# Block 0 of a retention layer prepared by pairs of heads, block 1's scores moved into the first product, and block 3's queries scaled on another engine

## The chip, the cores and the metric

The kernel runs on one core of one Trainium2 chip. The metric is the device time of one execution in microseconds (us). A core has a matrix engine (TensorE, PE in the profile; its weight loads are PEld), a vector engine (VectorE, DVE), a scalar engine (ScalarE, ACT), a general engine (GpSimd, POOL) and SyncE (SP), which here only issues DMAs. Each engine runs its instructions in the order in which they were written; between engines, semaphores make an instruction wait for its inputs.

## What is computed

A retention layer (attention without softmax, with a decay by distance) over 8 batches, 8 heads, 576 tokens and head size 64, and behind it a two-layer perceptron with `h * cos(h)` between its layers:

```python
scores = scale * np.matmul(q, k.transpose(0, 1, 3, 2))
gamma = 1.0 - 2.0 ** (-5.0 - np.arange(H, dtype=np.float32))
Dmat = np.where(rel >= 0, gamma[:, None, None] ** rel[None, :, :], 0.0)
attn = np.matmul(scores * Dmat[None], v)          # rel = query position - key position
x = attn.transpose(0, 2, 1, 3).reshape(B * S, H * D)   # 4608 x 512
h = x @ w_in                                      # 512 x 2048
out = (h * np.cos(h)) @ w_out                     # 2048 x 512
```

## The kernel before

The 4608 tokens are cut into 18 **blocks** of 256 (`BK`), numbered j. A **tile** n of the perceptron has 512 tokens, so blocks 2n and 2n+1. The decay is split into a factor for the query and one for the key (`gq`, `gkp`, `gkc`), so that a block needs a causal mask only, plus a running state `s_all` that carries key-times-value sums from earlier tokens. For one block the steps are:

- `load` (L132): q, k and v come as three float32 tiles `fq`, `fk`, `fv` by DMAs on SP's queue. The pool has three buffers of each.
- `scaled` (L163): one tensor-times-tensor per half y of the block multiplies q or k by its factors and rounds to bf16 (`qks`); `prep` (L188) does all four on POOL. `round_v` (L181) rounds v (`vb`).
- `turned` (L196) or, for blocks 0 and 1, `transpose_pe` (L218): PE turns `qks` into a PSUM bank, and ACT or DVE copies it out ("evacuates" it) to `qkT`.
- `scores` (L249): 32 small matmuls give query-key products in PSUM; two `masked` steps on DVE multiply them by the mask into `ret`.
- `sums_of` (L321): PE forms the key-value sums; the function that it returns adds them to the running state on DVE (`s_all`, L380 and L384), and the function which that one returns rounds the state on ACT (`sb`, L394).
- `out_own` (L404) and `out_carried` (L441): PE adds the block's own part (from `ret` and `vb`) and the carried part (from `sb`); ACT rounds the result to `xT`, the input of the perceptron.

The perceptron's first layer is `mm1` (L479): groups of PE matmuls h, a cosine on ACT (`cosh`, L503) and a multiplication on DVE (`gT`, L506). The dictionary `inside` (L924) names work that is put on PE's queue between such groups. For tile 0 the second layer is the loop at L988; for tiles 1 to 8 it is `mm2_seven` (L628), which saves one of eight quarter products by sums and differences of operands; `w_sums` (L518, `ws`) forms the differences of `w_out` on DVE, each 128x1024 in bf16, during tile 0's second layer.

The weights come by DMAs that POOL issues and that round float32 to bf16 on the way: `load_w_in` four times (512 columns each, L741), `load_w_out` four times (L747). `w_dma` numbers them 0 to 7, and `after` makes one DMA wait until another has landed.

**The order of the work is written by hand.** Three places matter here:

- The start, L760 to L870: loads of blocks 0 and 1 (v of block 1 waits until k of block 1 has landed, L763), tables and masks, block 0 up to `xT`, then block 1's transposes and its scores, and then the first product. `warm(n, tag)` (L232) puts n matmuls on zeros onto PE's queue to keep it busy. Block 2's loads wait for `w_dma[3]` (L846), and block 3's for `w_dma[6]` (L869).
- Tile 0's first layer, L891 to L937: eight groups of 16 matmuls. The second needs the second load of `w_in`, the third the third.
- Tile 0's second layer, L964 to L1002: `todo` lists work with the number of the matmul ahead of which it is queued, and is sorted by it. Number 28 is `turned(2)`, 34 to 36 are `ws` 6, 4 and 7 (first halves), 40 block 2's scores and masks, 41 its state, 42 `prep(3)`, 51 to 53 the second halves of the three `ws`, 54 `outputs(2)`, 55 the rounding of block 3's v on ACT, 60 `turned(3)`. Block 3's scores then stand inside tile 1's first product (L926).

Of the kernel before, what the change touches and what calls it, by code (L numbers as in the profile page):

```python
# [8 lines left out]
F32 = mybir.dt.float32  # L9
BF16 = mybir.dt.bfloat16  # L10
# [7 lines left out]
def kernel(  # L18
# [143 lines left out]

    def scaled(eng, j, name, y):  # L163
        f = tiles["f" + name, j]
        if ("qks", j) not in tiles:
            tiles["qks", j] = nat.tile([P, 2, 2, HG, 2, D], BF16, tag="qks", name="qks")
        dst = tiles["qks", j][:, "qk".index(name), y]
        if name == "q" or j < NP_B:
            src = f[:, :, y, :]
            by = (gq if name == "q" else gkp)[:, j % PERQ, y, :]  # L170
        else:
            src = f[:, y]
            by = gkc[:, (2 * j + y) % PERK, :]
        return eng.tensor_tensor(  # L174
            out=dst.rearrange("p b a d -> p a b d"),
            in0=src.rearrange("p (a b) d -> p a b d", a=2),
            in1=by.rearrange("p (a b) -> p a b", a=2).unsqueeze(3).to_broadcast([P, 2, HG, D]),
            op=ALU.mult,
        )
# [69 lines left out]
    def scores(j, banks):  # L249
        cs = chunks[j]  # L250
        kT = tiles["qkT", j]
        ret = retp.tile([P, 2, HG, 2, P], BF16, tag="ret", name="ret")
        if cs[0].pair:
            pss = [
                psum.tile([P, HG, 2, P], F32, tag=t, name="sc")
                if isinstance(t, str)
                else [psum.tile([P, HG, P], F32, tag=u, name="sc") for u in t]
                for t in banks
            ]
            order = [(c, y, he, hg) for hg in range(HG) for y in range(2) for he in range(2) for c in cs]  # L260
            mask = mask_p
            for c, y, he, hg in order:
                ps = pss[he]
                nc.tensor.matmul(
                    ps[y][c.rows, hg, :] if isinstance(ps, list) else ps[c.rows, hg, y, :],
                    lhsT=kT[he * D : he * D + D, 1, y, hg, c.rows],
                    rhs=q_cols(c, he, hg, c.n),
                    start=True,
                    stop=True,
                )  # L270

            def masked(he):
                if isinstance(pss[he], list):
                    for y in range(2):
                        nc.vector.tensor_tensor(
                            out=ret[:, he, :, y, :],
                            in0=pss[he][y],
                            in1=mask[:, y].unsqueeze(1).to_broadcast([P, HG, P]),
                            op=ALU.mult,
                        )  # L280
                    return
                nc.vector.tensor_tensor(  # L282
                    out=ret[:, he].rearrange("p b r i -> p b (r i)"),
                    in0=pss[he].rearrange("p b r i -> p b (r i)"),
                    in1=mask.rearrange("p r i -> p (r i)").unsqueeze(1).to_broadcast(
                        [P, HG, 2 * P]
                    ),
                    op=ALU.mult,
                )
# [28 lines left out]
        tiles["ret", j] = ret  # L318
# [442 lines left out]
    k1 = load(1, "k")  # L761
    load(1, "q")
    load(1, "v", gate=k1)  # L763
# [22 lines left out]
    warm(11, "n")  # L786
# [115 lines left out]

    def block1_sums():
        sums_of(1, "st")()()
# [16 lines left out]
    for n in range(NT):  # L921
        blocks = blocks_of.get(n) or [(e + k * E2, 0, W) for e in range(0, E2, 2) for k in range(2)]
        for i, (et, c0, cw) in enumerate(blocks):
            inside = {  # L924
                (0, 1): {2: block1_carried},
# [33 lines left out]
        if n == 0:  # L959
# [10 lines left out]
                (42, lambda: prep(3)),  # L970
# [17 lines left out]
            for done, (t, e) in enumerate(order):  # L988
# [9 lines left out]
                for u in range(2 * (t == 1) if t < 2 else 1) if e == ET - 1 else ():  # L998
# [3 lines left out]
                    stores.append((u * P, ot))  # L1002
            continue
# [115 lines left out]
```

## Time and profile before

| | |
|---|---|
| median of three runs | 296.96 us (296.85 to 297.02) |
| the profiled execution: its time, and its span in the profile | 296.85 us, 295.1 us |
| busy: PE, PEld, DVE, ACT, POOL | 284.5, 196.3, 215.2, 170.5, 143.4 us |
| chain of work that ended last, by engine | PE 83%, DVE 5%, ACT 3%, DMA 3%, POOL 2% |
| DMA, 10 to 30 us from the span's start | busy share 1.2 of 16 engines, about 205 to 255 GB/s |
| granted TensorE clock | 1.00 in every stretch |

The span is the stretch that the profile covers; about 1.75 us of the execution lie outside it. Times in the views below are counted from the span's start. A row of the timeline has the start, the length, the engine, the line, the operation, output and inputs, the number of instructions that it merges, and in brackets the idle time before it with what ended it. A row of DMA issues ends with the size and the time from issue to landing.

### The profile page before, as it was taken

To read this page: it belongs to the slowest core of one execution; us is meant where nothing else is said; L and a number is where in the kernel's file an instruction comes from. 1 tells how busy PE (TensorE), PEld (TensorE's weight loads), DVE (VectorE), ACT (ScalarE), POOL (GpSimd) and SP (SyncE) were. 2 spreads that over 40 slices of the span, in tenths; PEclk is the share of its full clock that TensorE was granted. 3 is DMA by queue.
4 is the path that set the end of the run, shared out by engine and by line. 5 is a ranking of instruction groups with operands and counts; after the bars stand their busy time and mean duration, and the time that the engine had idled before them with its cause. 6 is when DMAs were issued, how large, how long until landed. Compare 5 with 4: busy or idle time off the path is not lost.

```text
span 295.1 us, 10506 instructions
## 1 busy us (share of the span) xinstructions
PE 284.5 (96%) x4367; PEld 196.3 (67%) x4388; DVE 215.2 (73%) x300; ACT 170.5 (58%) x200; POOL 143.4 (49%) x163
## 2 busy tenths in 40 slices
PE   7899999999999999999999999999999999999994
PEld 2578545878864687468745884588458845884584
DVE  5756767758857887698769866986698669745943
ACT  3676317476558844767476737674768466535620
POOL 8621439970585995349434942495249014102400
PEclk9999999999999999999999999999999999999999
DMA  7999999999989857833873396429201130112013
GB/s 222 289 206 224 227 251 233 260 231 221 227 189 232 218 134 173 201 71 98 213 189 77 78 225 176 100 52 257 58 0 40 38 73 0 40 47 62 2 36 107
DMA packets 103981, 42.62 MB, mean 144 GB/s; under 512 B 68480, under 2 KB 103424, under 8 KB 103936
## 3 DMA queue, kind: packets, MB, share of 16 engines
q1 hardware_dynamic: 99184, 37.37, 51.8%
q0 software_dynamic: 4224, 4.19, 8.7%
q8 instruction: 36, 0.59, 0.9%
q10 hardware_dynamic: 528, 0.39, 0.4%
q14 instruction: 9, 0.07, 0.1%
HBM read 36.70 MB, written 9.44 MB: 156 GB/s over the span
## 4 chain that ended last, share of the span: by engine, by line
PE 83%; DVE 5%; ACT 3%; DMA 3%; POOL 2%; SPq 1%; issue 1%; ACTq 0%; DVEq 0%
PE h L490 41%; PE o L610 32%; PE ov L420 3%; PE tr L210 2%; POOL qks L174 2%; DMA fq<-in_q_dram 2%; PE ov L447 1%; PE sc L302 1%; DMA fk<-in_k_dram 1%; DVE gT L506 1%; PE st L335 1%; ACT cosh L503 1%; SPq L153 1%; DVE qks L174 1%; DVE ret L282 1%
## 5 line engine op out<-in xcount | busy, mean ns | idle before, releaser
L490 PE MATMUL h<-xT,w_in_sb 128*128 128x512 bf16 (+1 forms) x689 | 126.8, 340 | 1.3 <-DVE qkT L216 0.4
L506 DVE TENSOR_TENSOR gT<-h,cosh 128x1024 bf16<-128x1024 f32 x72 | 87.7, 1222 | 33.5 <-ACT cosh L503 33.1
L490 PEld LDWEIGHTS <-w_in_sb 128*128 128x128 bf16 x704 | 68.1, 98 | 55.2 <-issue 1.1
L503 ACT ACTIVATE cosh<-h,half_pi 128x1024 f32<-128x1024 f32 x72 | 79.9, 1115 | 40.5 <-PE h L490 40.5
L549 POOL TENSOR_TENSOR gs<-gT 128x512 bf16<-128x512 bf16 x28 | 35.8, 1277 | 100.4 <-DVE gT L506 100.4
L610 PEld LDWEIGHTS <-gs 128*128 128x128 bf16 x528 | 49.7, 98 | 5.9
L610 PEld LDWEIGHTS <-gT 128*128 128x128 bf16 x384 | 36.6, 98 | 6.1
L636 DVE TENSOR_TENSOR ot<-ot,o 128x512 f32<-128x512 f32 x35 | 23.2, 683 | 22.4 <-ACT ot L640 14.2
L174 POOL TENSOR_TENSOR qks<-fk,gkc 128x512 bf16<-128x512 f32 x32 | 37.1, 1178 | 2.8 <-DMA fk<-in_k_dram 2.8
L174 POOL TENSOR_TENSOR qks<-fq,gq 128x512 bf16<-128x512 f32 x31 | 34.7, 1137 | 7.5 <-DMA fq<-in_q_dram 7.5
L216 ACT COPY qkT<-tr 128x1024 bf16<-128x1024 bf16 x29 | 27.7, 1022 | 6.4 <-PE tr L210 6.4
L394 ACT CAST sb<-s_all 128x768 bf16<-128x768 f32 (+2 forms) x18 | 16.3, 904 | 25.6 <-DVE s_all L384 21.6
L610 PE MATMUL o<-w_out_sb,gs 128*128 128x256 bf16 (+1 forms) x264 | 30.6, 269 | 0.1
L610 PE MATMUL o<-w_out_sb,gT 128*128 128x256 bf16 x256 | 30.6, 273 | 0.0
L610 PE MATMUL o<-ws,gs 128*128 128x256 bf16 (+1 forms) x264 | 30.5, 269 | 0.0
L640 ACT COPY ot<-o 128x512 f32<-128x512 f32 x33 | 19.3, 584 | 16.0 <-PE o L610 16.0
L311 DVE TENSOR_TENSOR ret<-sc,mask_c 128x512 bf16<-128x512 f32 x32 | 20.7, 685 | 7.3 <-PE sc L302 7.3
L185 POOL CAST vb<-fv 128x512 bf16<-128x512 f32 x31 | 19.3, 646 | 4.8 <-DMA fv<-in_v_dram 4.8
L466 ACT CAST xT<-ov 128x1024 bf16<-128x1024 f32 x16 | 16.2, 1012 | 9.4 <-PE ov L447 9.2
L384 DVE TENSOR_TENSOR s_all<-st,s_all 128x256 f32<-128x256 f32 x49 | 20.7, 422 | 1.2
L549 DVE TENSOR_TENSOR gs<-gT 128x512 bf16<-128x512 bf16 (+1 forms) x25 | 16.7, 668 | 0.5
L610 PE MATMUL o<-ws,gT 128*128 128x256 bf16 x128 | 15.3, 273 | 0.0
(73 smaller groups left out, 207.0 us busy)
## 6 DMA issues: line engine op xcount, KB each, us to landing
out_dram<-ot SPq DMA_DIRECT2D x68, 128.0 KB, 2.6
fk<-in_k_dram SPq DMA_DIRECT2D x28, 256.0 KB, 4.9
fv<-in_v_dram SPq DMA_DIRECT2D x28, 256.0 KB, 4.8
fq<-in_q_dram SPq DMA_DIRECT2D x12, 512.0 KB, 5.1
w_in_sb<-in_moe_w_in_dram POOLq DMA_DIRECT2D x4, 512.0 KB, 8.0
w_out_sb<-in_moe_w_out_dram POOLq DMA_DIRECT2D x4, 512.0 KB, 8.3
fq<-in_q_dram SPq DMA_DIRECT2D x4, 384.0 KB, 5.1
fk<-in_k_dram SPq DMA_DIRECT2D x2, 512.0 KB, 4.9
```

What stands on the lines that cost most here:

```text
L174: return eng.tensor_tensor(out=dst.rearrange("p b a d -> p a b d"), in0=src.rearrange("p (a b) d -> p a b d", a=2), in1=by.rearrange("p (a ...
L185: runs[y](vb[:, y], f[:, :, y, :] if j < NP_B else f[:, y])
L216: evacs[r](tiles["qkT", j][:, :, :, :, r * HP : r * HP + HP], pss[r])
L311: nc.vector.tensor_tensor(out=ret[:, he].rearrange("p b y i -> p (b y) i"), in0=ps[he].rearrange("p b y i -> p (b y) i"), in1=mask_c.unsqu ...
L384: nc.vector.tensor_tensor(out=s32[:, u], in0=ps[c.half][:, c.y], in1=s32[:, u - 1] if u else tiles["run"], op=ALU.add,)
L490: nc.tensor.matmul(ps[:, j, :], lhsT=w_in_sb[:, dg, (et + j) * P : (et + j + 1) * P], rhs=xT[:, dg, c0 : c0 + w], start=(dg == 0), stop=(d ...
L503: nc.scalar.activation(cosh, ps, ACTF.Sin, bias=half_pi, scale=1.0)
L506: nc.vector.tensor_mul(gT[:, et : et + m, c0 : c0 + w], ps, cosh)
L549: i = eng.tensor_tensor(out=tiles["gs", n, x][:, e : e + step], in0=a[:, e : e + step], in1=b[:, e : e + step], op=op_,)
L610: nc.tensor.matmul(dst[i], lhsT=lhs[:, e, j * P : (j + 1) * P], rhs=rhs[:, e, c0:c1], start=(fresh and e == 0 and (i == 0 or len(parts) > 2)),
L636: return lambda: nc.vector.tensor_tensor(out=out_, in0=in0, in1=in1, op=ALU.add)
L640: held.append(lambda ps=tiles["all", x]: nc.scalar.copy(t, ps))
```

## The change

It has these parts:

- **Block 0 by pairs of heads.** `scaled` and `transpose_pe` are replaced for block 0 by `scaled_heads` and `turned_heads`, which handle two of the four head columns hg at a time: eight multiplications of 128x256 on DVE instead of four of 128x512, four evacuations that are all on ACT (before, three on ACT and one on DVE). `scores` takes a range of head columns, so that 16 matmuls and two masks of 128x512 follow the first pair, and the same the second. Half of block 0's v is rounded on POOL instead of ACT.
- **Loads whole.** v of block 1 no longer waits for k of block 1. Block 2's loads wait for the third load of `w_in` (`w_dma[2]`) instead of the fourth.
- **Block 1.** Its scores and masks stand in the first product, behind its first four matmuls, instead of ahead of it. Its four transposes come after `out_own(0)` and `out_carried(0)`, but for the first; two evacuations change engine.
- **Fillers.** `warm` is called for 9 + 2 + 1 matmuls instead of 11 + 2 + 3 + 2 + 2.
- **Block 3.** Its two q multiplications go to DVE (number 42 of the list); POOL keeps those of k.
- **Two `ws`** (4 and 7, second halves) move from numbers 52 and 53 to the end of tile 0's second layer.
- Paths of `scores` and `prep` that nothing takes are removed.

The diff, cut to its core:

```diff
+    def scaled_heads(eng, name, g):
+        if ("qks", 0) not in tiles:
+            tiles["qks", 0] = nat.tile([P, 2, 2, HG, 2, D], BF16, tag="qks", name="qks")
+        dst = tiles["qks", 0][:, "qk".index(name), :, 2 * g : 2 * g + 2]
+        f = tiles["f" + name, 0].rearrange("p (a b) r d -> p r b a d", a=2)[:, :, 2 * g : 2 * g + 2]
+        by = (gq if name == "q" else gkp)[:, 0].rearrange("p r (a b) -> p r b a", a=2)
+        for y in range(2):
+            eng.tensor_tensor(
+                out=dst[:, y],
+                in0=f[:, y],
+                in1=by[:, y, 2 * g : 2 * g + 2].unsqueeze(3).to_broadcast([P, 2, 2, D]),
+                op=ALU.mult,
+            )
+
+    def turned_heads(name, g, bank, evac=nc.scalar.copy):
+        if ("qkT", 0) not in tiles:
+            new_qkT(0)
+        m = "qk".index(name)
+        ps = psum.tile([P, 2, 2, P], BF16, tag=bank, name="tr")
+        for y in range(2):
+            for u in range(2):
+                nc.tensor.transpose(
+                    ps[:, y, u, :],
+                    tiles["qks", 0][:, m, y, 2 * g + u].rearrange("s a d -> s (a d)"),
+                    ident,
+                )
+        evac(tiles["qkT", 0][:, m, :, 2 * g : 2 * g + 2], ps)
...
-    def prep(j):
-        for name in "kq" if j < NP_B else "qk":
+    def prep(j, eng_q=nc.gpsimd):
+        for name in "qk":
             for y in range(2):
-                scaled(nc.gpsimd, j, name, y)
+                scaled(eng_q if name == "q" else nc.gpsimd, j, name, y)
...
-    def scores(j, banks):
+    def scores(j, banks, g0=0, g1=HG):
...
-            order = [(c, y, he, hg) for hg in range(HG) for y in range(2) for he in range(2) for c in cs]
+            order = [
+                (c, y, he, hg) for hg in range(g0, g1) for y in range(2) for he in range(2) for c in cs
+            ]
...
                 nc.vector.tensor_tensor(
-                    out=ret[:, he].rearrange("p b r i -> p b (r i)"),
-                    in0=pss[he].rearrange("p b r i -> p b (r i)"),
+                    out=ret[:, he, g0:g1].rearrange("p b r i -> p b (r i)"),
+                    in0=pss[he][:, g0:g1].rearrange("p b r i -> p b (r i)"),
...
     load(0, "kqv")
-    k1 = load(1, "k")
-    load(1, "q")
-    load(1, "v", gate=k1)
+    load(1, "kqv")
...
-    warm(11, "n")
+    warm(9, "b")
...
-    scaled(nc.vector, 0, "k", 0)
-    scaled(nc.vector, 0, "k", 1)
-    transpose_pe(0, "k", "n", act, (0,))
-    transpose_pe(0, "k", "st", act, (1,))
-    scaled(nc.vector, 0, "q", 0)
-    scaled(nc.vector, 0, "q", 1)
-    transpose_pe(0, "q", "a", act, (0,))
-    transpose_pe(0, "q", "b", vec, (1,))
+    scaled_heads(nc.vector, "k", 0)
+    turned_heads("k", 0, "n")
+    scaled_heads(nc.vector, "k", 1)
+    turned_heads("k", 1, "m")
+    scaled_heads(nc.vector, "q", 0)
+    turned_heads("q", 0, "st")
+    scaled_heads(nc.vector, "q", 1)
+    masks = scores(0, "ab", 0, 2)
+    turned_heads("q", 1, "n")
     w_dma = [load_w_in(0)]
-    round_v(0, (act, act))
+    for masked in masks:
+        masked()
     warm(2, "m")
-    for masked in scores(0, "ab"):
+    masks = scores(0, "ab", 2, HG)
+    round_v(0, (nc.gpsimd.tensor_copy, act))
+    for masked in masks:
         masked()
+    warm(1, "m")
     sums_of(0, "st")()()
     scaled(nc.gpsimd, 1, "k", 0)
-    warm(3, "m")
-    transpose_pe(1, "k", "n", act, (0,))
+    transpose_pe(1, "k", "n", vec, (0,))
     scaled(nc.gpsimd, 1, "k", 1)
     w_dma += [load_w_in(e) for e in (512, 1024, 1536)]
-    load_next(names="kqv", gate=w_dma[3])
+    load_next(names="kqv", gate=w_dma[2])
     ps0 = psum.tile([P, DG, BK], F32, tag="m", name="ov")
     out_own(0, ps0)
     scaled(nc.vector, 1, "q", 0)
     scaled(nc.vector, 1, "q", 1)
-    transpose_pe(1, "k", "st", vec, (1,))
     out_carried(0, ps0)
     act(x_of(0), ps0)
+    transpose_pe(1, "k", "st", vec, (1,))
+    transpose_pe(1, "q", "a", act, (0,))
+    transpose_pe(1, "q", "b", vec, (1,))
     nc.scalar.activation(sine, half_pi, ACTF.Sin, bias=0.0, scale=1.0)
     round_v(1, (act, nc.gpsimd.tensor_copy))
-    warm(2, "n")
-    transpose_pe(1, "q", "a", vec, (0,))
-    transpose_pe(1, "q", "b", vec, (1,))
-    warm(2, "n")
-    for masked in scores(1, "ab"):
-        masked()
...
+    def block1_scores():
+        for masked in scores(1, "ab"):
+            masked()
...
             inside = {
+                (0, 0): {1: block1_scores},
                 (0, 1): {2: block1_carried},
...
-                (42, lambda: prep(3)),
+                (42, lambda: prep(3, nc.vector)),
...
-                    (51, 6, 4), (52, 4, 4), (53, 7, 4),
+                    (51, 6, 4), (99, 4, 4), (99, 7, 4),
...
+            for _, late in todo:
+                late()
             continue
```

More of the change, by code (lines that the diff above doesn't have):

```diff
@@ L247, in ov_cols @@
         return cols.rearrange("p (r i) -> p r i", r=2)[:, :, c.i0 : c.i0 + n]
-    def scores(j, banks):
+    def scores(j, banks, g0=0, g1=HG):
         cs = chunks[j]
         kT = tiles["qkT", j]
-        ret = retp.tile([P, 2, HG, 2, P], BF16, tag="ret", name="ret")
+        if not g0:
+            tiles["ret", j] = retp.tile([P, 2, HG, 2, P], BF16, tag="ret", name="ret")
+        ret = tiles["ret", j]
         if cs[0].pair:
[L254 to L258, printed above, removed]
-            ]
-            order = [(c, y, he, hg) for hg in range(HG) for y in range(2) for he in range(2) for c in cs]
-            mask = mask_p
+            if not g0:
+                tiles["sc", j] = [psum.tile([P, HG, 2, P], F32, tag=t, name="sc") for t in banks]
+            pss = tiles["sc", j]
+            order = [
+                (c, y, he, hg) for hg in range(g0, g1) for y in range(2) for he in range(2) for c in cs
+            ]
             for c, y, he, hg in order:
-                ps = pss[he]
                 nc.tensor.matmul(
-                    ps[y][c.rows, hg, :] if isinstance(ps, list) else ps[c.rows, hg, y, :],
+                    pss[he][c.rows, hg, y, :],
                     lhsT=kT[he * D : he * D + D, 1, y, hg, c.rows],
@@ L272, in masked @@
             def masked(he):
[L273 to L281, printed above, removed]
                 nc.vector.tensor_tensor(
-                    out=ret[:, he].rearrange("p b r i -> p b (r i)"),
-                    in0=pss[he].rearrange("p b r i -> p b (r i)"),
-                    in1=mask.rearrange("p r i -> p (r i)").unsqueeze(1).to_broadcast(
-                        [P, HG, 2 * P]
+                    out=ret[:, he, g0:g1].rearrange("p b r i -> p b (r i)"),
+                    in0=pss[he][:, g0:g1].rearrange("p b r i -> p b (r i)"),
+                    in1=mask_p.rearrange("p r i -> p (r i)").unsqueeze(1).to_broadcast(
+                        [P, g1 - g0, 2 * P]
                     ),
@@ L316, in masked @@
                 )
-        tiles["ret", j] = ret
+            tiles["ret", j] = ret
         return [lambda: masked(0), lambda: masked(1)]
```

## The prediction

> **What bounds the kernel now.** I read the busy row first (PE 284.5 of 295.1 us), then the chain of waits (PE 83% of it): whatever does not make PE wait is free. The waits of PE by engine show none over 0.4 us after 20 us, so PE can be freed of little there; it can only be made to wait more. So two stretches count: the start, until the first product runs without a break at 20.33, and 38 to 53 us, where the chain leaves PE for DMA, POOL and ACT. I read each engine's timeline in both, and the landings in the view of DMA issues.
>
> The start: PE's timeline, and the DMA issues of the second and third loads of `w_in` (issued at 11.41 and 12.20; the last column is the time to landing):
>
> ```profile
> 15.52 1.92 PE L490 MATMUL h<-xT,w_in_sb 128*128 128x256 bf16 x16
> 18.11 0.95 PE L420 MATMUL ov<-ret,vb 64*64 64x128 bf16 x32
> 19.00 1.05 PE L490 MATMUL h<-xT,w_in_sb 128*128 128x256 bf16 x8
> 20.33 9.89 PE L490 MATMUL h<-xT,w_in_sb 128*128 128x256 bf16 x89
> ```
>
> ```profile
> w_in_sb<-in_moe_w_in_dram POOLq DMA_DIRECT2D x1, 512.0 KB, 7.2
> ...
> w_in_sb<-in_moe_w_in_dram POOLq DMA_DIRECT2D x1, 512.0 KB, 8.9
> ```
>
> The second group of the product starts at 19.00; its weights landed at 11.41 + 7.2 = 18.6. It has eight matmuls left at 20.33 (0.109 each), so the third group starts at 21.2; its weights landed at 12.20 + 8.9 = 21.1. **PE already arrives as the weights do.** The DMA engines are full from 3 us on (share over 1.1 in every microsecond), and the same six loads of blocks 0 and 1 and two of `w_in` stand ahead of the third in either order. So the start can give 0.1 us, however much faster block 0 becomes.
>
> The middle, by engine (PE from 44, ACT from 44, POOL from 39, DVE from 40 us):
>
> ```profile
> 45.41 0.66 PE L447 MATMUL ov<-qkT,sb 64*64 64x64 bf16 x24
> 46.22 1.24 PE L991 MATMUL o<-w_out_sb,gT 128*128 128x512 bf16 x5 [0.16 <-issue]
> 48.27 0.29 PE L210 MATMUL tr<-ident,qks 64*128 64x64 bf16 x8 [0.35 <-POOL qks L174]
> 50.84 0.63 PE L302 MATMUL sc<-qkT 64*64 64x64 bf16 x32
> ```
>
> ```profile
> 44.83 0.83 ACT L394 CAST sb<-s_all 128x768 bf16<-128x768 f32 x1 [5.30 <-DVE s_all L384]
> 46.12 1.01 ACT L466 CAST xT<-ov 128x1024 bf16<-128x1024 f32 x1 [0.46 <-PE ov L447]
> 47.03 1.14 ACT L185 CAST vb<-fv 128x512 bf16<-128x512 f32 x2
> 48.07 1.08 ACT L1001 COPY ot<-o 128x512 f32<-128x512 f32 x2
> 49.03 1.95 ACT L216 COPY qkT<-tr 128x1024 bf16<-128x1024 bf16 x2
> ```
>
> ```profile
> 39.87 0.61 POOL L185 CAST vb<-fv 128x512 bf16<-128x512 f32 x1 [1.76 <-DMA fv<-in_v_dram]
> 43.28 2.04 POOL L174 TENSOR_TENSOR qks<-fq,gq 128x512 bf16<-128x512 f32 x2 [2.80 <-DMA fq<-in_q_dram]
> 45.28 2.94 POOL L174 TENSOR_TENSOR qks<-fk,gkc 128x512 bf16<-128x512 f32 x2
> ```
>
> ```profile
> 40.17 1.58 DVE L529 TENSOR_TENSOR ws<-w_out_sb,ws 128x1024 bf16<-128x1024 bf16 x2
> 41.66 0.68 DVE L529 TENSOR_TENSOR w_out_sb<-w_out_sb 128x1024 bf16<-128x1024 bf16 x1
> 42.27 1.28 DVE L311 TENSOR_TENSOR ret<-sc,mask_c 128x512 bf16<-128x512 f32 x2
> 43.91 0.88 DVE L384 TENSOR_TENSOR s_all<-st,s_all 128x256 f32<-128x256 f32 x2
> 44.71 2.60 DVE L529 TENSOR_TENSOR ws<-w_out_sb,ws 128x1024 bf16<-128x1024 bf16 x2
> 47.24 1.53 DVE L529 TENSOR_TENSOR w_out_sb<-w_out_sb 128x1024 bf16<-128x1024 bf16 x1
> ```
>
> Here one chain has no slack. DVE works without a gap from 39.56: three `ws`, block 2's masks, its state (ends 44.79); ACT rounds the state at 44.83; PE's carried part waits for it; then ACT runs without a gap from `xT` at 46.12 to the second evacuation of block 3 (50.98), for which block 3's scores on PE wait. **What delays the `ws` on DVE delays the end.** The same rows show what can: beside POOL's multiplications a `ws` takes 1.3 to 1.5 us (2.60 for two, 1.53), beside an idle POOL 0.68; and POOL's own take 1.47 (2.94 for two) instead of 1.02. They take turns: each waits for the other's to end.
>
> **Part by part.**
>
> *Block 0 by head pairs.* Two masks of 1024 columns take 2.36 us with 1.22 for the last, so 1.14 apiece; two of 512 take 1.28 with 0.68, so 0.60. That is 1.04 ns a column and 0.065 fixed: the four extra multiplications and two extra masks cost 0.4 us, and DVE gives up one copy of 0.42. The gain is overlap: the first pair's scores can start at about 8.2 instead of 8.67, masks end at 11.4 instead of 11.77, `xT` 12.9 instead of 13.39. Behind it PE no longer does block 1's scores first, so the product could start at about 13.9 instead of 15.52. Block 1's scores then wait for their evacuations (14.45): PE scores 14.55, two masks to 17.6 (2.35 as now), `out_own(1)` 17.65 to 18.55, and there it meets the weights (18.6, then 21.1): gain 0.1 at most.
>
> *v of block 1 ungated* moves ahead of the first `w_in` in time of issue: from 9.26 to about 6.2, where POOL issues `w_in` at 7.02 (lands 13.2). 512 KB at the 348 GB/s of those microseconds are 1.5 us. Bounds: `w_in` keeps 13.2 (start term 0), or lands at 14.7. In that case product 14.8, scores 15.35, masks 16.05 to 18.4, `out_own(1)` to 19.35: second group 0.35 late. I take 0.2, between them: block 2's k was issued at 23.66 and landed only after the two loads of `w_out` issued before it, which speaks for order of issue, but the two issues here overlap. The Trainium skill ("DMA: Bandwidth & Descriptors", Queues, rings and completion order) has each DMA engine take turns between queues by packets; by that rule the first `w_in` would keep its place, and the start term would be 0.
>
> *Fillers* fall into waits of PE; 0. *Block 2's loads* are issued from 21.1 instead of 23.66 into engines that are full (share 1.2) until about 27; bounds 0 and 2.6 us earlier; q of block 2, which DVE awaits for 0.49 before 35.95, may come earlier, and no PE wait hangs on it; 0.
>
> *q of block 3 to DVE.* Two of 0.69 behind the state, ahead of `ws` 6; done about 46, or 48 with the delay below. The stall of 0.35 at 48.27 goes. What is late next is ACT: its evacuations follow its own queue from 46.12, so PE waits the 0.35 at block 3's scores. Gain 0 (bounds 0 and 0.35).
>
> *k of block 3 on POOL.* This is the step that decides. Before, POOL waited from 40.48 to 43.28 for q of block 3 and so left the three `ws` alone. Now k is next in POOL's queue. It was issued from 33.49 with 7.3 us to landing: 40.8 (its second half: issue ended 38.18, so about 41 to 43). So: `ws` 6 ends about 41.0; POOL's first k takes 0.95 to 41.95; `ws` 4 to 42.55; POOL's second k to 43.5; `ws` 7 to 44.1. Masks start at 44.05 instead of 42.27: **1.8 us late**, with two turns lost. One turn lost is 0.9; none is 0. Behind it: state 46.6, rounding 46.6 to 47.45, carried part 47.5 instead of 45.71, ACT's row from 47.9, block 3's scores 52.8 instead of 51.0. Nothing of the delay is hidden. I take 1.8, since the row 44.71 to 48.76 shows just that turn-taking with the same instructions.
>
> *Two `ws` at the end* fall on DVE after 50.26, where it idles 1.25 before block 3's masks: 1.3 us alone, 2.9 beside POOL. Masks 0 to 1.3 late; I take 0, since PE comes 1.8 later by then and POOL is through with part of block 4.
>
> Sum against the profiled execution's 296.85 (span 295.1 and 1.75 outside): 0.2 for the start, 1.8 for the middle, less 0.15 as a later `ws` 6 no longer meets POOL's cast at 39.87 (its 1.58 for two against 1.28 shows 0.3): 1.85, so **298.7**. The median of the runs is 296.96, 0.1 above that execution. After 64 us no wait of PE over 0.5 is left that could swallow the shift.
>
> **Rivals.**
>
> 1. *POOL's k misses the `ws`* (not slower). It decides by the landing of k: if its first half lands after 42.3, 1.5 us later than now, or the pair is done before 40.2, DVE loses no turn. POOL cannot begin it before block 2's v (40.48), which speaks against the second. Then only the start's 0 to 0.35 is left: 296.8 to 297.2.
> 2. *Faster.* The start gives the 0.5 of `xT` after all because the weights land earlier, and the 0.35 stall is not met again on ACT: 296.0. Against it: full DMA engines from 3 us and ACT's row without a gap.
> 3. *A slow start.* One queue's share of `w_in` lands another microsecond late, or PE runs at half rate into the product: the fillers take 0.43 us apiece at first (11 in 4.87), the same shape 0.22 later (27 in 6.21). Sixteen matmuls of the first group would cost 1.7 more, so with the forecast's middle 300.2. The Trainium skill ("TensorE: Matmul & The Clock Gate", Part 1) wants about 3.4 us of sustained work inside a free-running window; nine fillers make 3.84 us against 4.7 for eleven, so by it this case is possible, and no run here shows it yet.
>
> **Numbers.** Forecast 0.55 (its own range 297.7 to 299.2, one turn or two lost), rival 1 0.27, rival 2 0.10, rival 3 0.08. The range 296.7 to 299.3 leaves out rivals 2 and 3. What a measurement of this kernel can tell from no change is about 0.2%, 0.6 us: slower 0.55 + 0.08 and a little of rival 1's upper end, 0.64; same 0.26; faster 0.10.
>
> **What would show it.** Right: POOL's k of block 3 next to `ws` 4 and 7 on DVE between 41 and 44, each over 1.2 us; masks of block 2 near 44; PE waiting before its carried part; the stall at `turned(3)` gone and one before block 3's scores. The first `w_in` landing between 13.2 and 14.8, the third group of the product at or after 21.1. Wrong: masks of block 2 still near 42.3; a third group before 21; block 3's scores before 51.

## The result, and the profile after

The changed kernel takes **299.52 us** (median of 20 runs, 297.82 to 301.22); the kernel before, on the same chip, 296.95 (20 runs, 19 of them between 296.65 and 297.52). The ratio is 1.0077 (95% interval 1.0055 to 1.0098): slower by about 2.3 us (the medians lie 2.57 apart). The profiled execution took 300.35, span 298.6. The forecast was 298.7, slower; it fell 0.8 short of the median, which lies 0.2 above the end of the range of 296.7 to 299.3. By the ratio, on the median of 296.96 that was known before, the changed kernel takes 299.25, just inside that range.

The page of the changed kernel: its span, the busy row, the granted TensorE clock in slices of 7.5 us, and the shares of the chain that ended last.

```profile
span 298.6 us, 10518 instructions
...
PE 287.4 (96%) x4380; PEld 197.3 (66%) x4380; DVE 217.8 (73%) x307; ACT 170.6 (57%) x200; POOL 141.5 (47%) x162
...
PEclk9599999999999999999999999999999999999999
...
PE 82%; DVE 8%; ACT 4%; DMA 3%; issue 1%; POOL 0%; DVEq 0%; ACTq 0%
```

PE is busy 2.9 us longer than before (284.5) with 4380 matmuls in the records (4367 before; some records can be missing). That is not the loss by itself: 1.0 of it lies after 87 us, where both kernels take the same time within 0.2. But 1.3 lies ahead of the second product `gT` on DVE (19.3 us busy before, 20.6 after), where PE idles no longer than before: there matmuls take longer. The 5 in the clock's row says where: the second slice ran in part at half clock. In the page of before that row has nines throughout. **The granted clock differs from run to run**: of the 20 runs of the changed kernel 16 have a mean granted clock of 0.994 or less, two have 1.0, and these two are the fastest, 297.82 and 297.88. The other two read 0.998; the mean leaves out the time ahead of the clock's first record, so a clock that comes up late hardly shows in it (number 4).

To see where the 3.5 us between the two profiled spans come from, I followed one instruction that both kernels have 72 times, DVE's product `gT`, and took its start in the changed kernel less its start in the kernel before (worked out from the two traces; spans 298.6 and 295.1):

```
gT number         2nd    9th    14th   17th   72nd
before, at us     22.56  53.25  67.10  87.08  279.99
after, later by   1.07   2.37   2.31   3.35   3.46
```

So 1.07 is lost by the time the first product runs without a break, 1.24 in the middle, 1.04 between 67 and 87 us, and 0.1 later.

**The start.** The changed kernel's PE, answering the four lines of before (the third group of the product started at 21.2 there, the second at 19.00):

```profile
15.53 0.60 PE L508 MATMUL h<-xT,w_in_sb 128*128 128x256 bf16 x4
...
16.67 1.48 PE L508 MATMUL h<-xT,w_in_sb 128*128 128x256 bf16 x12
...
19.18 0.95 PE L438 MATMUL ov<-ret,vb 64*64 64x128 bf16 x32 [0.29 <-DVE ret L300]
20.07 1.05 PE L508 MATMUL h<-xT,w_in_sb 128*128 128x256 bf16 x8
```

The product starts as late as before (15.52), though block 0's work was to be through 1.6 us sooner, and its second group is 1.07 late. The weights are not the cause. The second and third load of `w_in`, issued at 11.41 and 12.21, land after 6.6 and 8.4 us, at 18.0 and 20.6 (18.6 and 21.1 before), and PE comes for the third at 22.3: at 21.39 it has eight matmuls of the second group left, 0.109 each.

```profile
w_in_sb<-in_moe_w_in_dram POOLq DMA_DIRECT2D x1, 512.0 KB, 6.6
...
w_in_sb<-in_moe_w_in_dram POOLq DMA_DIRECT2D x1, 512.0 KB, 8.4
```

The stretches of 2 us show why; columns are the window, its length, busy us and instructions of PE, of its weight load, of DVE, ACT and POOL, then the granted clock, DMA share and GB/s. After:

```profile
4.00:6.00 2.00, 1.73 (x7) 0.38 (x5) 1.17 (x4) 0.17 (x1) 1.84 (x7) 1.00 1.15 347
6.00:8.00 2.00, 1.17 (x9) 0.56 (x9) 1.78 (x6) 1.68 (x3) 1.16 (x3) 1.00 1.15 347
8.00:10.00 2.00, 1.87 (x24) 0.90 (x24) 1.29 (x2) 0.91 (x3) 1.08 (x2) 0.59 1.15 344
10.00:12.00 2.00, 2.00 (x45) 1.33 (x47) 1.29 (x2) 0.27 (x1) 2.00 (x3) 0.50 1.23 226
...
14.00:16.00 2.00, 2.00 (x32) 1.58 (x24) 1.34 (x3) 1.51 (x2) 0.88 (x2) 0.70 1.25 239
```

Before, the stretches 6 to 8 and 8 to 10 us:

```profile
6.00:8.00 2.00, 1.46 (x18) 1.03 (x18) 1.56 (x3) 1.30 (x3) 1.92 (x3) 1.00 1.15 347
8.00:10.00 2.00, 1.81 (x68) 1.20 (x65) 1.01 (x2) 1.29 (x3) 0.58 (x1) 1.00 1.15 348
```

PE had 2.90 us of work in 4 to 8 us instead of 3.46, with nine fillers ahead instead of eleven and none between the turns of the head pairs; then the clock is at half from 8.38 to 15.20, two periods of 3.41 us. The column of the clock also reads 1.00 where the trace has no record of it yet: up to 4.96 us in the changed kernel, 6.0 in the kernel before. There PE runs at half too, as a filler takes 0.43 us and later 0.22; so "1.00 in every stretch" for the kernel before holds from 6.0 us on.

**The middle.** DVE, POOL, PE and ACT of the changed kernel:

```profile
41.23 2.71 DVE L547 TENSOR_TENSOR ws<-w_out_sb,ws 128x1024 bf16<-128x1024 bf16 x2
43.86 0.68 DVE L547 TENSOR_TENSOR w_out_sb<-w_out_sb 128x1024 bf16<-128x1024 bf16 x1
44.46 1.28 DVE L329 TENSOR_TENSOR ret<-sc,mask_c 128x512 bf16<-128x512 f32 x2
...
46.90 1.28 DVE L202 TENSOR_TENSOR qks<-fq,gq 128x512 bf16<-128x512 f32 x2
...
52.09 1.40 DVE L547 TENSOR_TENSOR ws<-w_out_sb,ws 128x1024 bf16<-128x1024 bf16 x1
53.41 1.09 DVE L547 TENSOR_TENSOR w_out_sb<-w_out_sb 128x1024 bf16<-128x1024 bf16 x1
54.42 1.27 DVE L329 TENSOR_TENSOR ret<-sc,mask_c 128x512 bf16<-128x512 f32 x2
```

```profile
40.90 2.49 POOL L202 TENSOR_TENSOR qks<-fk,gkc 128x512 bf16<-128x512 f32 x2 [1.89 <-DMA fk<-in_k_dram]
48.90 2.04 POOL L202 TENSOR_TENSOR qks<-fq,gq 128x512 bf16<-128x512 f32 x2 [5.51 <-PE o L1012]
50.90 2.04 POOL L202 TENSOR_TENSOR qks<-fk,gkc 128x512 bf16<-128x512 f32 x2
```

```profile
46.48 0.21 PE L465 MATMUL ov<-qkT,sb 64*64 64x64 bf16 x4
47.91 0.35 PE L465 MATMUL ov<-qkT,sb 64*64 64x64 bf16 x20 [1.22 <-ACT sb L412]
...
49.59 0.64 PE L238 MATMUL tr<-ident,qks 64*128 64x64 bf16 x32
...
51.63 1.47 PE L508 MATMUL h<-xT,w_in_sb 128*128 128x256 bf16 x12 [0.43 <-DVE ot L1022]
53.03 0.63 PE L320 MATMUL sc<-qkT 64*64 64x64 bf16 x32
...
56.88 0.45 PE L353 MATMUL st<-vb,qks 64*64 64x64 bf16 x32 [0.50 <-DVE gT L524]
```

```profile
47.02 0.83 ACT L412 CAST sb<-s_all 128x768 bf16<-128x768 f32 x1 [6.43 <-DVE s_all L402]
48.31 1.01 ACT L484 CAST xT<-ov 128x1024 bf16<-128x1024 f32 x1 [0.46 <-PE ov L465]
...
51.22 1.95 ACT L244 COPY qkT<-tr 128x1024 bf16<-128x1024 bf16 x2
```

POOL's k of block 3 runs from 40.90 to 43.39, beside the `ws`: two `ws` take 2.71 where two alone take 1.28 to 1.4, the third runs alone in 0.68. (POOL's two rows from 48.90 are block 4's.) Masks are at 44.46, 2.19 after those of before; 1.07 of that came from the start, 1.12 is the middle's own. PE waits 1.22 us in the middle of the carried part for ACT's rounding, and block 3's scores are at 53.03, again 2.19 late. Nothing is hidden on the way.

**After 67 us.** One gap is of another kind: PE stands still for 0.88 us at 82 us and waits for nothing that the profile shows.

```profile
82.81 1.81 PE L628 MATMUL o<-w_out_sb,gs 128*128 128x256 bf16 x15 [0.88 <-issue]
```

### The profile page after: what moved, and what is told of

The parts are those of the page before. It is cut to its first block, busy times and chain, and to the rows that moved or that the text cites. A ratio compares the mean times of both kernels' runs of the same rounds, so it can differ in the third digit from the quotient of the medians.

```text
span 298.6 us, 10518 instructions
## 1 busy us (share of the span) xinstructions
PE 287.4 (96%) x4380; PEld 197.3 (66%) x4380; DVE 217.8 (73%) x307; ACT 170.6 (57%) x200; POOL 141.5 (47%) x162
## 4 chain that ended last, share of the span: by engine, by line
PE 82%; DVE 8%; ACT 4%; DMA 3%; issue 1%; POOL 0%; DVEq 0%; ACTq 0%
PE h L508 37%; PE o L628 31%; PE ov L438 3%; PE tr L238 2%; PE o L1012 2%; PE ov L465 2%; DVE gT L524 2%; DMA fk<-in_k_dram 1%; DMA fv<-in_v_dram 1%; PE st L353 1%; DVE ret L329 1%; PE sc L320 1%; DVE ws L547 1%; ACT qkT L244 1%; DVE s_all L402 1%
## 5 line engine op out<-in xcount | busy, mean ns | idle before, releaser
L654 DVE TENSOR_TENSOR ot<-ot,o 128x512 f32<-128x512 f32 x35 | 23.2, 683 | 22.7 <-ACT ot L658 14.2
L202 POOL TENSOR_TENSOR qks<-fq,gq 128x512 bf16<-128x512 f32 x29 | 31.6, 1109 | 9.6 <-PE o L1012 5.5
L329 DVE TENSOR_TENSOR ret<-sc,mask_c 128x512 bf16<-128x512 f32 x32 | 20.6, 684 | 6.0 <-PE sc L320 5.0
L213 POOL CAST vb<-fv 128x512 bf16<-128x512 f32 x32 | 21.3, 688 | 2.7 <-DMA fv<-in_v_dram 2.7
```

The lines of the kernel that those rows point to most:

```text
L202: return eng.tensor_tensor(out=dst.rearrange("p b a d -> p a b d"), in0=src.rearrange("p (a b) d -> p a b d", a=2), in1=by.rearrange("p (a ...
L213: runs[y](vb[:, y], f[:, :, y, :] if j < NP_B else f[:, y])
L329: nc.vector.tensor_tensor(out=ret[:, he].rearrange("p b y i -> p (b y) i"), in0=ps[he].rearrange("p b y i -> p (b y) i"), in1=mask_c.unsqu ...
L654: return lambda: nc.vector.tensor_tensor(out=out_, in0=in0, in1=in1, op=ALU.add)
```

## The experiments

Theory A: two separate causes, DVE and POOL taking turns at the `ws` (1.1 to 1.2 us) and a TensorE clock that falls to half where PE waits at the start (about 1). Rival B: all of it comes from the middle. Rival C: all of it from the start's new order. Each result is set against runs of the kernel before on the same chip: for the first four 297.30 (27 runs), for the next four 297.83 (33), for the last four 297.55 (35).

**1. The start alone.** The changed kernel with block 3 put back:

```
-                (42, lambda: prep(3, nc.vector)),
+                (42, lambda: prep(3)),
-                    (51, 6, 4), (99, 4, 4), (99, 7, 4),
+                    (51, 6, 4), (52, 4, 4), (53, 7, 4),
```

> The changed kernel with block 3 put back: its q multiplications on POOL, and the second halves of ws 4 and 7 at numbers 52 and 53. So the start of the change alone. Theory A (two causes: turn-taking of POOL and DVE at the ws, worth 1.1 to 1.2 us in the changed profile, and a TensorE clock that falls back to half between 8.4 and 15.2 us, worth about 1 us where it happens): some 1.1 us less than the changed kernel, so about 298.3, and still slower than before by 0 to 2 us with the runs spread widely, the ones with full granted clock near 296.9. Theory B (everything comes from the middle): no slower than before, 296.9, with a narrow spread. Theory C (everything comes from the start): as the changed kernel, 299.5.

Measured: 298.38 us (297.10 to 300.45, 10 runs), ratio 1.0037 (1.0005 to 1.0070). The two runs with a granted clock of 1.0 took 297.10 and 297.44. Its profile has the clock at half from 8.63 to 15.46; `gT` number 2 is 1.18 late, number 9 is 1.01. The start costs about a microsecond: B falls. That it does so through the clock is tested by number 5.

**2. Block 3 alone.** The kernel before with `prep(3, nc.vector)` and the two `ws` at the end, its start untouched.

> The kernel before with only block 3's q on DVE and the two ws second halves at the end. The middle of the change alone. Theory A: 1.1 to 1.9 us slower than before, 298.1 to 298.8, with as narrow a spread as before has, since the start is not touched: POOL's k of block 3 next to ws 4 and 7, masks of block 2 at 43.4 or later instead of 42.3. Theory B: 299.5, the whole loss. Theory C: 296.9, no change.

Measured: 299.38 (298.83 to 300.89, 6 runs), ratio 1.0081 (1.0057 to 1.0105). C falls: the middle alone is as slow as the whole change. The time is what B had forecast and 0.6 above A's range; B is out by number 1, and A had not reckoned with the clock here. DVE and PE of this run, and the 3.4 us on either side of 47.4 us (columns as above):

```profile
40.23 2.39 DVE L529 TENSOR_TENSOR ws<-w_out_sb,ws 128x1024 bf16<-128x1024 bf16 x2
42.54 1.53 DVE L529 TENSOR_TENSOR w_out_sb<-w_out_sb 128x1024 bf16<-128x1024 bf16 x1
43.99 1.27 DVE L311 TENSOR_TENSOR ret<-sc,mask_c 128x512 bf16<-128x512 f32 x2
```

```profile
47.44 0.48 PE L447 MATMUL ov<-qkT,sb 64*64 64x64 bf16 x20 [1.34 <-ACT sb L394]
48.25 2.34 PE L991 MATMUL o<-w_out_sb,gT 128*128 128x512 bf16 x5 [0.33 <-issue]
```

```profile
44.00:47.40 3.40, 1.65 (x41) 0.70 (x39) 3.33 (x8) 0.83 (x1) 0.00 (x0) 1.00 0.84 209
47.40:50.80 3.40, 3.03 (x37) 1.36 (x40) 1.18 (x3) 2.71 (x5) 1.91 (x2) 0.50 1.15 254
```

Here two turns are lost: the second and the third `ws` run beside POOL's k (the first meets POOL's rounding of v, as before), and the masks are 1.72 late (the forecast said 1.8, at 44.05). Then one cause sets off the other: PE waits so long for the state that it is busy 1.65 of 3.4 us, and the clock falls to half for the next period, five matmuls taking 2.34 instead of 1.24. In three of the six runs the granted clock reads 0.994, which is one such period; the two that read 1.0 took 298.83 and 299.37. In the whole change the middle's loss is smaller (1.12 at the masks), as DVE comes 1.07 later, when POOL's first k has been running for 0.33 us, and no `ws` meets the rounding of v. So the two costs do not add up: 1.0037 and 1.0081 apart, 1.0077 together.

**3. Fillers.** The changed kernel with seven more fillers in PE's waits of the start:

```
     turned_heads("k", 0, "n")
+    warm(2, "b")
...
     turned_heads("k", 1, "m")
+    warm(2, "b")
...
     turned_heads("q", 0, "st")
+    warm(3, "b")
```

> The changed kernel with seven more matmuls on zeros on PE, two behind the transposes of k's first pair, two behind the second's, three behind those of q's first pair, all in waits of PE. If the clock falls back because PE works only some 60% of the stretch from 5 to 8.4 us, the granted clock stays at full from about 5 us on in most runs, the product's first group starts about 1 us earlier than in the changed profile (14.5 instead of 15.5), and the median falls by about 1 to 1.5 us, to 298 to 298.5, with a narrower spread. If the start is late for its loads and the clock costs nothing, the median stays at 299.5 although the clock is full.

Measured: 298.26 (297.55 to 300.31, 12 runs), ratio 1.0026 (1.0000 to 1.0053); 11 of 12 runs within 297.55 to 298.67. More work for PE made the kernel faster by 0.5%. The same stretches as above (in this run the clock has its first record at 7.23 us, and up to there PE runs at half, so the rows ahead of it show more busy time for the same work; in the period behind it, 7.23 to 10.64, PE is busy 81%):

```profile
4.00:6.00 2.00, 1.96 (x8) 0.63 (x7) 1.31 (x4) 0.17 (x1) 1.89 (x6) 1.00 1.15 346
6.00:8.00 2.00, 2.00 (x13) 1.15 (x12) 1.73 (x5) 1.17 (x2) 1.56 (x4) 1.00 1.15 347
8.00:10.00 2.00, 1.60 (x24) 0.90 (x24) 0.83 (x2) 1.13 (x3) 1.06 (x2) 1.00 1.15 347
```

`gT` number 2 is now 0.23 late, and what is left is the middle: one turn, masks 0.9 late with the start's 0.23.

```profile
40.40 1.41 DVE L547 TENSOR_TENSOR ws<-w_out_sb,ws 128x1024 bf16<-128x1024 bf16 x2
41.72 1.53 DVE L547 TENSOR_TENSOR w_out_sb<-w_out_sb 128x1024 bf16<-128x1024 bf16 x1
43.17 1.28 DVE L329 TENSOR_TENSOR ret<-sc,mask_c 128x512 bf16<-128x512 f32 x2
```

**4. The `ws` behind the state.** The changed kernel with the three first halves later, so that no `ws` stands ahead of block 2's masks:

```
-                    (2, 5, 0), (8, 5, 4), (34, 6, 0), (35, 4, 0), (36, 7, 0),
+                    (2, 5, 0), (8, 5, 4), (43, 6, 0), (44, 4, 0), (45, 7, 0),
```

> The changed kernel with the first halves of ws 6, 4 and 7 moved behind block 2's masks, its state and block 3's q (numbers 43 to 45 instead of 34 to 36). Nothing on DVE then takes turns with POOL's k of block 3 ahead of the state. Theory A: the 1.1 us of the middle goes, and up to 0.4 more, since the masks no longer stand behind 2 us of ws and wait for the scores alone: median 297.9 to 298.4, the start's spread stays. If the turns are not what makes the state late, masks still start 2 us after those of before and the median stays at 299.5.

Measured: 298.16 (296.89 to 300.44, 12 runs), ratio 1.0043 (1.0014 to 1.0073), in two heaps: four runs from 296.89 to 297.35 and five from 299.84 to 300.44. The profiled run is one of the upper heap (300.08). The turn is gone in it, the masks wait for their scores alone; but its clock is full only from 17.41 us on, `gT` number 2 is 2.09 late. The mean granted clock of that run reads 0.998, since it counts no time before the clock's first record.

**5. Start at full clock.** Number 1 and number 3 together: block 3 put back, seven fillers.

> The changed kernel with the middle put back (block 3's q on POOL, the two late ws at their old places) and with seven fillers in PE's waits of the start. Theory A (two causes: DVE and POOL taking turns at the ws, and a TensorE clock that falls to half where PE waits at the start): the clock stays full, the middle is that of before, so only the start's own term is left, third group of the product at 21.3 to 21.6, 296.9 to 297.4 us, few runs over 298. Rival B (all of it from the middle): 296.6 to 297.2 as well, but then the same kernel without the fillers (298.38 median) should have given that too. Rival C (the new order of the start is slower by itself, clock or not): 298 to 298.5, as without the fillers.

Measured: 297.17 (296.63 to 299.56, 11 runs), ratio 0.9983 (0.9952 to 1.0015). The new order of the start costs nothing that can be told once the clock holds; without the fillers the ratio was 1.0037. What it gives depends on when the clock gets full: in this run and number 3, where that is at 7.0 and 7.2 us, `gT` number 2 is 0.18 and 0.23 late; where it is at 4.7, 5.0 and 6.2 (numbers 7, 9, 11, with the same start) it is 0.30, 0.22 and 0.16 early. Since the phase of the periods differs from run to run, the plainest comparison is of runs in which they begin alike: in the changed kernel (from 4.96) PE was busy 64% of the first period at full clock, and the clock fell; in number 9 (from 4.99, with the fillers) 89%, and in number 8 (from 4.82, with the start of before) 73%, and it stayed.

**6. Fewer fillers before.** The kernel before with nine instead of eleven ahead, two instead of three, and without the other four; nothing else.

> The kernel before with fewer fillers at the start and nothing else changed: nine instead of eleven ahead, two instead of three, and none instead of two and two. Theory A: PE has waits of the size that the changed kernel has, so in a good part of the runs the clock falls to half for one or two windows of 3.41 us between 6 and 17 us, each half-rate window costs some 1 us: median 297.5 to 299, spread from 296.8 to 300. Rival C (the new order itself is slow): the order is the old one, so 296.7 to 297.3 with the narrow spread of before.

Measured: 297.55 (296.86 to 298.74, 11 runs), ratio 1.0006 (0.9987 to 1.0026). The clock falls, as theory A has it: the profiled run has it at half from 7.47 to 10.88 after PE was busy 55% of a period, and six of the eleven runs have a granted clock of 0.992 to 0.994. They took 297.23 to 298.36, the other five 296.86 to 298.74. So a half-rate period costs less than I had said: 0.43 at the start (`gT` number 2), and nothing that the median shows, since in the old order PE waits for DVE in that period anyway. Fewer fillers explain that the clock falls; that it costs a microsecond takes the new order too, in which two periods are at half. (The same profile is 1.3 late at `gT` number 9, by a wait of 1.16 for block 3's q on POOL, whose load came late in this run.)

**7. The `ws` moved, with fillers.** Number 3 and number 4, and the second halves in the next tile's first product:

```
-                    (51, 6, 4), (99, 4, 4), (99, 7, 4),
...
+            if n == 1 and i in (2, 4):
+                for x in (6, 4) if i == 2 else (7,):
+                    w_sums(x, 4, E2)
```

> The changed kernel with the seven fillers, the first halves of ws 6, 4, 7 behind block 2's state (places 43 to 45), and the second halves of all three in the next tile's first product (behind its third and fifth group), where DVE idles 2 us and POOL is nearly through. Theory A: no ws stands ahead of block 2's masks or of block 3's masks, so both turns of the middle go, masks of block 2 wait for their scores alone, PE's wait for gT before the state of block 3 (0.64) goes: 296.5 to 297.2, with few runs over 298. Rival B' (what the middle loses is not the turns at the ws but block 3's scores waiting for q on DVE and ACT's row): 298.0 to 298.5, as with the fillers alone.

Measured: 297.03 (296.58 to 298.06, 11 runs), ratio 0.9982 (0.9965 to 0.9999). `gT` number 9 is 0.56 ahead of before, number 14 is 0.11 behind: the moved `ws` make DVE late for one of its evacuations, and PE waits where it waited 0.4.

```profile
64.11 4.53 PE L508 MATMUL h<-xT,w_in_sb 128*128 128x256 bf16 x40 [1.07 <-DVE qkT L244]
```

**8. The same middle with the start of before**, without fillers of mine.

> The kernel before with block 3's q on DVE as in the change, and the ws halves moved as in the run beside it. Start as before, so its clock stays full. Theory A: 2.4 us less than the middle's part of the change alone (299.38): 296.3 to 297.0, perhaps 0.2 to 0.4 below the kernel before, since the stall of 0.35 ahead of block 3's transposes goes and no ws meets POOL. Rival B': 298.5 to 299.4.

Measured: 297.39 (296.88 to 299.73, 11 runs), ratio 0.9976 (0.9942 to 1.0009): no gain that can be told from none, and 0.4 to 1.1 us above what I expected. In the profiled run (298.22, clock full from 4.82) DVE stands idle 2.05 us for block 3's q, which landed later here:

```profile
46.49 1.29 DVE L174 TENSOR_TENSOR qks<-fq,gq 128x512 bf16<-128x512 f32 x2 [2.05 <-DMA fq<-in_q_dram]
```

**9. The late `ws` apart.** As number 7, but 6 at the end of tile 0, 4 behind block 3's sums, 7 behind the next tile's fifth group.

> The changed kernel with the seven fillers; ws 6, 4, 7 first halves behind block 2's state; and the three second halves apart, each into one idle stretch of DVE: 6 at the end of tile 0's second product (1.5 us idle before block 3's masks), 4 behind block 3's sums (2.1 us idle before the next gT), 7 behind the fifth group of the next tile (1.0 idle). Theory A (what is left of the loss is DVE arriving late at something PE waits for): the wait of PE for DVE's qkT, 1.07 us at 64 us where the run with the ws in the next tile lost 0.67, goes back to 0.4, the rest is as there: 0.5 to 0.7 below that run, 296.0 to 296.5 us, and 0.3 to 0.6 below the kernel before on the same chip. Rival B'' (that wait is ACT's row, not DVE's): no gain, 296.7 to 297.1.

Measured: 297.06 (296.30 to 298.91, 12 runs), ratio 0.9984 (0.9962 to 1.0006). The wait went back to 0.40 as expected, `gT` numbers 9 and 14 are both 0.16 ahead of before; but the median did not move and lies 0.6 above A's range, in that of the rival. A tenth or two in one place are under what these runs scatter by.

**10. The same with the start of before.**

> The kernel before with block 3's q on DVE and the ws halves placed as in the run beside it: the change's middle without its start. Theory A: at or below the kernel before by 0 to 0.3 us, 296.6 to 297.0, and 0.3 above the run beside it, whose start brings the product's weights 0.3 earlier. If block 3's q lands as late as in the earlier run of this kind (46.5 us), 0.8 more, 297.4 to 297.8.

Measured: 297.19 (296.41 to 298.27, 12 runs), ratio 0.9995 (0.9973 to 1.0016), 0.2 above what I expected. No turn ahead of block 2's masks, no loss, and no gain that can be told.

**11. Fillers, and the `ws` behind the state** (number 3 and number 4 together).

> The changed kernel with the seven fillers and the three first halves of the ws behind block 2's state; the late halves stay at the end of tile 0's second product as in the change. It parts the two terms of the middle. Theory A: the fillers alone gave 298.26 with 0.93 lost to the turn at the ws and 0.25 to 0.3 to the late ws ahead of block 3's masks; the turn goes, and the late ws, now next to POOL's k of block 4, cost 0.3 to 0.7: 297.0 to 297.6, with few runs at 299.8 to 300.4, where the run of the same kernel without the fillers had five of twelve. Rival B (the far runs near 300 come from the middle, not from the start's clock): again a third or more of the runs at 299.8 to 300.4.

Measured: **297.12** (296.15 to 297.39, 12 runs), ratio 0.9976 (0.9955 to 0.9997). All twelve runs lie within 1.24 us, and the upper heap of number 4 is gone: it came from the clock at the start. Masks now wait for their scores alone, and the late `ws` show as PE's wait of 0.66 for `gT` (0.34 before):

```profile
41.78 1.29 DVE L329 TENSOR_TENSOR ret<-sc,mask_c 128x512 bf16<-128x512 f32 x2 [1.68 <-PE sc L320]
```

```profile
54.45 0.45 PE L353 MATMUL st<-vb,qks 64*64 64x64 bf16 x32 [0.66 <-DVE gT L524]
```

**12. The gate alone.** The kernel before with `gate=w_dma[2]` for block 2's loads.

> The kernel before with block 2's loads issued one load of the first weights earlier, as in the change, and nothing else. The forecast priced this at 0. If it holds: the same as before within 0.2 us in median and spread. Rival: block 2's q and k land 2 to 3 us earlier and with them block 3's loads, whose late landing makes runs of the kernel before long at full clock: then median and spread fall below the kernel before on the same chip by 0.2 to 0.8 us.

Measured: 297.24 (296.57 to 297.93, 12 runs), ratio 0.9986 (0.9961 to 1.0011). Its 12 runs scatter less than the 35 of the kernel before on that chip (296.55 to 301.09), but the interval does not exclude no change. In its profile half of block 2's q landed earlier, at 31.82 (33.76 before), but block 3's q at 43.24 (43.21): what the rival needed did not happen in that run. It stays open whether the earlier loads save the runs that are long at full clock.

**What follows.** Theory A stands for the start and the middle, 2.3 of the 3.46 us of the profiled run. From the changed kernel, fillers in PE's waits take away half a per cent (1.0077 to 1.0026), and moving three `ws` behind the state another half (1.0026 to 0.9976); each takes away its own cause in the profile. The changed kernel with both is no slower than the kernel before, and by its interval 0.03 to 0.45% faster; of several intervals one that ends so near to 1 is not a gain to count on. What is not settled is the scatter of the kernel before at full clock, and PE's gap without a releaser: 0.88 us in the changed kernel, `gT` number 17 later by another 0.4 in numbers 2, 11 and 12, by 0.2 or nothing in the others.

## Why the prediction was right, and where it was not

- **"What delays the `ws` on DVE delays the end"** held, step by step: POOL's k began at 40.90 (forecast about 41.0), masks moved, the state, the rounding, the carried part and block 3's scores moved with them by the same 2.19. The size was off in the whole change: 1.8 was forecast, 1.12 was lost at the masks and 1.24 in all. The two `ws` beside POOL's k took 2.71 us instead of 1.4, as DVE came when POOL's first k was already running; with block 3 alone the loss was 1.72. The range had one turn in it. The masks, with one input from PSUM, are not held up: in number 11 two of them take 1.29 beside POOL's k (41.15 to 43.19), as alone. The Trainium skill ("SBUF — State Buffer", SBUF: two separate sides) has a DVE operation with two inputs from SBUF and a GpSimd operation shut each other out for a whole instruction; these rows agree.
- **"Fillers fall into waits of PE; 0"** is the step that failed. They fill waits, and by that they hold the clock. With twelve of them instead of twenty, and block 0 in short turns, PE was busy 64% of the period from 4.96 to 8.38 us, the clock fell for two periods, and the second group of the first product came 1.07 late. The second half of rival 3 is what happened, at a chance of 0.08, in most runs. I priced it as a clock that comes up late; it came up in time and fell back. With both terms as measured the sum is 296.85 + 1.07 + 1.24 = 299.2, near the median. It leaves out the 1.04 between 67 and 87 us, for which the forecast had no term and the runs show no cause.
- **That the total came near is in part luck.** The middle was forecast 0.56 too dear (1.8 against 1.24) and the start 0.87 too cheap (0.2 against 1.07); the two errors partly cancel, and the start's cause was not the one that the forecast named.
- **The start otherwise: 0.2, bounds 0 to 0.35.** At full clock it lay between 0.30 gained and 0.23 lost. The product began at 14.2 to 14.7 (forecast 13.9), and the third load of `w_in` landed at 20.6 to 21.05 (21.1 before), so that it could give 0.3, not 0.1.
- **v ungated: `w_in` keeps 13.2 or lands at 14.7; 0.2 between them.** `w_in` landed at 14.10, 0.85 later, and v at 15.07, though both were issued within 0.2 us (6.11 and 6.28): they shared the time, neither took it all. The Trainium skill ("DMA: Bandwidth & Descriptors", Queues, rings and completion order) has each DMA engine take turns between queues by packets, and these landings agree with it. But that the first `w_in` would then keep its place, as the prediction has it, does not follow: two transfers that share by turns both take longer, here 8.0 us from issue to landing for `w_in` instead of 6.2.
- **q of block 3 to DVE: 0.** The stall at its transposes went (49.59, no wait), and the new wait came, 0.43 for DVE's copy of the output ahead of the product rather than at the scores. ACT's row ahead of it was the cause named.
- **Two late `ws`: 0, bounds 0 to 1.3.** They cost 0.1 to 0.3: PE's wait for `gT` at the state of block 3 grew from 0.34 to 0.50 (0.66 in number 11).
- **Block 2's loads: 0** is neither shown nor refuted (number 12).

## What to carry to other kernels

When an edit takes fillers out or makes PE's early work shorter, add up what PE does in each few microseconds of the start, not only its waits: a wait that costs nothing by itself can cost the clock. Count it as matmul work rather than as busy time (next section), as small matmuls keep PE busy with little work. Price a pair of engines that take turns by counting which instructions stand next to each other, and give the range for one more and one fewer, since a shift of 1 us elsewhere changes the count. Put long operations of the contended kind behind, not ahead of, what PE waits for next.

## What the runs showed of the hardware

- In the 14 profiled runs the granted clock fell to half four times between its first rise and the last matmuls, each time for one or two periods of 3.41 us, and each time after a period in which PE was busy 50 to 67% (1.65 of 3.4 us in number 2). The Trainium skill ("TensorE: Matmul & The Clock Gate", Part 1) gives an idle window of about 3.4 us for the fall; here windows that were half to two thirds busy were enough.
- Busy time does not decide it alone. After eight other periods of 52 to 66% the clock stayed full: 61% at 45.92 us in the changed kernel, 66% in number 6, and six at the end of a kernel, such as 55% from 289.31 us in the kernel before. Nor does the clock always come back after a busy period: in the changed kernel it stayed at half through one with PE busy throughout (8.38 to 11.79), in number 1 likewise (8.63 to 12.05), and in number 4 through two of 97% and 98%.
- What parts them is the matmul work. Count a matmul as the rows times the columns of its weights times the columns that it streams, with a filler (`128*128` weights, 512 columns) as 1; a matmul of `64*64` and 64 columns is then 1/32. All 12 periods after which the clock fell, eight of them at the end of a kernel, hold at most 5.95 fillers' worth, and all 1164 after which it stayed full at least 6.60. Of 26 periods at half clock (those ahead of the first record counted in), the 8 after which it stayed at half hold at most 5.91, the 18 after which it rose at least 6.03. The changed kernel held 4.06 from 4.96 to 8.38, then 5.91 and 6.27; number 4, whose clock came so late, at most 5.84 in each period up to 14.0; number 8 held 7.97 and number 9 10.79 in the same place. So by these traces a period keeps or brings full clock with about six fillers' worth of work. This was worked out from the traces afterwards; no run was made to test it.
- The kernel before, too, scatters from chip to chip: 19 of 20 runs within 0.9 us on the first, from 296.7 to 300.4 at full clock on that of numbers 5 to 8.
